# Attention and two feed-forward layers: k's parts, q's low part and a sum placed in other blocks, v's load behind k's moves, and one step of a weight's conversion a block sooner

## The chip, the cores and the metric

One Trainium2 chip, of which the program uses one core. The metric is the time of one launch in microseconds of device time, median of several runs. A core has TensorE (PE; its weight loads are PEld), VectorE (DVE), ScalarE (ACT), GpSimd (POOL) and SyncE (SP, which here only issues DMAs). Each works off its own list of instructions in order, and waits where an operand is not there yet.

## What is computed

Clustered attention over 2 x 8 heads of 768 positions and 64 dimensions: queries and keys get the nearest of 16 centroids, a query sees only the keys of its own centroid. Two feed-forward parts follow.

```python
mask = q_assign[:, :, :, None] == k_assign[:, :, None, :]
scores = np.where(mask, scale * np.matmul(q, k.transpose(0, 1, 3, 2)), -1000000000.0)
attn = softmax(scores)                      # exp(s - max) / (sum + 1e-9)
x = np.matmul(attn, v)                      # -> (1536, 512)
x = ((x @ w1) * (x @ w2)) @ w3 @ w_out
out = (sigmoid(x @ w_gate) * (x @ w_val)) @ w_out2
```

## The kernel before

Everything runs as float32 split in a high and a low part (`hi` and `lo`, in the engine's fast float32 format), so that a product takes two or three passes. The weights are loaded as raw words and rebuilt in several steps (`f64_steps`, "conversion"), each step on another engine.

The attention part is one loop over 48 blocks (L580 to L706). A block is 256 queries of one head; `i` counts blocks, six to a pair of heads, three a head. `pr` is the pair (0 to 7) and `at` the block in it (0 to 5). `nxt` is pair `pr + 1`, `later` is `pr + 2` (none from pr = 6 on). The order of all engines is the order of this code: the scheduler leaves it alone, so a call's place in the loop is its place in its engine's list.

In one turn PE computes the scores `s` of a later block (L339, twice), turns the exponentials of block i (`pt`, L372, three times) and multiplies block i - 1 with v (`av`, L413 with the high part `ph`, L414 with the low part `pl`, in three groups k2 = 0, 1, 2). DVE takes the maxima `nm` (L351) and most of the `pl` (L401). ACT takes the exponentials `e` (L362), the `ph` (L390) and copies `av` to `xa` (L422, `take_x`); all blocks share one `av`, so the next block's products wait for this copy. In blocks 0, 1, 2 and 4 ACT only copies `pt` to `pc` for k2 = 0 (L387) and POOL makes `ph` and `pl` from it (L54, L59).

Between these stand the steps that prepare the next pairs. They are bound to blocks by `if` lines:

- `load_qk(later)` at block 0; `raw` is q and k of a pair. `prep_split` (L185) makes four tiles of it: `hi0` (q, ACT, L192) at block 3, `lo0` (q, DVE, L194), `hi1` (k, ACT, L56) and `lo1` (k, POOL, L59) at block 4. Each has one buffer, which the pair before uses too.
- `prep_scatter` moves rows of them by DMA into the operands QH, KH, QX and KX: for the pair's first head at block 5 of `later`'s turn, for the second at block 1 of `nxt`'s turn, there behind `load_v(nxt)`.
- `join_x` (blocks 0 and 1) moves the halves of the last pair's result by DMA, `add_x` (POOL, L466, block 3) adds them, `spread` reads the sums' inverses `r` back by DMA, `norm_x` and `split_x` (POOL, block 5) finish x.
- The mask of the next pair: DVE turns the one-hot matrix (`ohT`, L282, end of block 2), and at block 3 eight small DMAs carry it into QH and KH (`prep_mask`). Behind them SP issues the two DMAs of `spread`.

The first-layer weights `w_0_0` and `w_0_1` are converted inside the attention part. `steps[1]` is that of `w_0_1`; its first step issues the load of `w_f` (L88), its second is a DVE operation on what was loaded (`w_a`, L100), then ACT, POOL and DVE again. `loads` (L656) and `CONVERT` (L572) say in which block (pr, at) a step is written: the load in (6, 4), the DVE step in (6, 5), the rest in pair 7.

Of the kernel before, what the change touches and what calls it, by code (L numbers as in the profile page):

```python
# [8 lines left out]
F32 = mybir.dt.float32  # L9
# [18 lines left out]
def tile_cluster_attention__then__moe__then__gated_moe(  # L28
# [22 lines left out]
    def split(x, hi, lo, hi_engine, lo_engine):  # L51

        if hi_engine is nc.gpsimd:
            nc.gpsimd.tensor_scalar(out=hi, in0=x, scalar1=1.0, scalar2=1.0, op0=ALU.mult, op1=ALU.mult)  # L54
        elif hi_engine is nc.scalar:
            nc.scalar.copy(hi, x)  # L56
        else:
            nc.vector.tensor_copy(hi, x)
        lo_engine.tensor_tensor(out=lo, in0=x, in1=hi, op=ALU.subtract)  # L59

    def move(dst, src):
        nc.sync.dma_start(dst.bitcast(F32), src.bitcast(F32))
# [109 lines left out]
    def load_v(pr, e=None):  # L172
        if e != 1:
            raw[pr, "v"] = core.tile([128, 2, KT, D], F32, tag="vraw", name=f"vraw{pr}", bufs=1)
        which = slice(0, 2) if e is None else slice(e, e + 1)
        nc.sync.dma_start(raw[pr, "v"][:, which], v[pr][:, which])
# [5 lines left out]

        return nc.vector if pr == 0 else nc.gpsimd

    def prep_split(pr):  # L185
        hl = []
        for w in range(2):
            t = raw[pr, w]
            hi = core.tile([128, S], F32R, tag="hi", name=f"hi{pr}_{w}", bufs=2)
            lo = core.tile([128, S], F32R, tag="lo", name=f"lo{pr}_{w}", bufs=2)  # L190
            if w == 0:
                nc.scalar.activation(hi, t, AF.Copy, scale=0.125)  # L192
                yield
                nc.vector.scalar_tensor_tensor(out=lo, in0=t, scalar=0.125, in1=hi.bitcast(F32), op0=ALU.mult, op1=ALU.subtract)  # L194
            else:
                split(t, hi, lo, nc.scalar, nc.vector if pr == 0 else nc.gpsimd)
            hl += [hi, lo]
        opnd[pr, "hl"] = hl

    def prep_split_1_hi(w):  # L200

# [22 lines left out]
    def prep_scatter_hi(pr, e):  # L224
        qh, ql, kh, kl = opnd[pr, "hl"]
        r = slice(64 * e, 64 * e + 64)
        QH, KH, QX, KX = operands(pr, e)
        move(QH[0:64], qh[r])
        move(KH[0:64], kh[r])
        move(QX[0:64], qh[r])  # L230
        move(KX[64:128], kh[r])

    def prep_scatter_lo(pr, e):
        qh, ql, kh, kl = opnd[pr, "hl"]
# [144 lines left out]
    def split_hi(i, k2):  # L379
        if (i, k2) not in pts:  # L380
            return
        pt = pts[i, k2]
        ph = core.tile([128, 2, 256], F32R, tag="ph", name=f"ph{i}_{k2}", bufs=4)
        pl = core.tile([128, 2, 256], F32R, tag="pl", name=f"pl{i}_{k2}", bufs=4)
        if by_pool(i, k2):
            pc = core.tile([128, 2, 256], F32, tag="pc", name=f"pc{i}", bufs=1)
            nc.scalar.copy(pc, pt)  # L387
            pts[i, k2] = pc
        else:
            nc.scalar.copy(ph, pt)  # L390
        phs[i, k2] = (ph, pl)
# [43 lines left out]
    def invert(pr):  # L435

        ss = acc_x[pr, "sum"]
        nc.vector.reciprocal(ss, ss)
# [133 lines left out]
    CONVERT = {}  # L572
    for n, slots in enumerate((
        ((0, 3), (0, 3), (0, 5), (1, 0), (1, 0), (1, 1)),
        ((6, 5), (7, 0), (7, 1), (7, 2), (7, 3), (7, 4)),
    )):
        for slot in slots:
            CONVERT.setdefault(slot, []).append(n)
    if True:
        for i in range(-2, NB + 2):  # L580
            pr, at = divmod(i, 6)
            nxt = pr + 1 if 0 <= i and pr + 1 < NPR else None
            later = nxt + 1 if nxt and nxt + 1 < NPR else None

            scores(2 * i + 3)
            if i == -1:
                warm(11, "warm3")
            split_hi(i - 1, 2)
            transposes(i, 0)
            if i == NB - 1:  # L590
                turn_sums(pr, ps_s.tile([128, 1024], F32, tag="s", name=f"rp{pr}")[:, 0:128])
            maxima(2 * i + 3)
            if i == 0:
                prep_code(0, 1)
                prep_onehot(0, 1)
                prep_turn(0, 1)
                prep_sims(1)
                prep_sum(1)
            if i == NB - 1:
                store_sums(pr)  # L600
            if later and at == 0 and pr:
                load_qk(later)
            if at == 0 and 0 < pr and i < NB:
                join_x(pr - 1, 0)
            if at == 1 and 0 < pr and i < NB:
                join_x(pr - 1, 1)
            if nxt and nxt > 1 and at == 1:
                load_v(nxt)
                prep_scatter_hi(nxt, 1)
                if nxt > 2:  # L610
                    prep_scatter_lo(nxt, 1)
            if nxt and at == 3:
                for e in range(2):
                    if nxt == e == 1:
                        prep_scatter(1, 1)
                    prep_mask(nxt, e)
                    if nxt == 2 and e == 0:
                        prep_scatter_lo(2, 1)
            split_lo(i - 1, 2)
            split_hi(i, 0)  # L620
            split_lo(i, 0)
            if i == 0:
                next(split_1_lo, None)
                prep_v(0, 1)
            if nxt and at == 1:
                prep_argmax(nxt)
            if nxt and at == 2:
                prep_onehot(nxt)
            if 0 < pr and i < NB and at == 5:
                norm_x(pr - 1)  # L630
                split_x(pr - 1)
            if nxt == 1 and at == 2:
                load_v(nxt)
            if 0 < pr and i < NB and at == 3:
                add_x(pr - 1)
                spread(pr - 1, "xb", 1)
            exponentials(2 * i + 3)
            if i == -1:
                next(split_1_lo)
                prep_argmax(0, 1)  # L640
                load_qk(2)
            if 0 <= i < NB and at == 4:
                guard_sums(pr)
            if later and at == 3:
                halves = prep_split(later)
                next(halves)
            if later and at == 4:
                for _ in halves:
                    pass
            weighted_v(i - 1, 0)  # L650
            weighted_v(i - 1, 1)
            if i == 1:
                prep_scatter(1, 0)
            if later and at == 5:
                prep_scatter(later, 0)
            loads = ((6, 4), (7, 1), (7, 3))  # L656
            if (pr, at) in loads:
                convert(1 + loads.index((pr, at)))

            similar = later if at == 5 else None  # L660
            if similar:
                prep_sims(similar)
            scores(2 * i + 4)
            turning = 0 <= i < NB - 1 and at == 5
            if turning:
                turn_sums(pr, sps[2 * i + 4][:, S : S + 128])
            if nxt and at == 1:
                prep_code(nxt)
            if 0 < pr < NPR and at == 0:
                prep_v(pr, 1)  # L670
            if nxt and at == 3:
                prep_v(nxt, 0)
            transposes(i, 1)
            split_hi(i, 1)
            weighted_v(i - 1, 2)
            transposes(i, 2)
            if i == NB:
                convert(2)
            take_x(i - 1)
            if i == NB:  # L680
                convert(3)
            if i == 0:
                prep_mask(0, 1)
            if similar:
                prep_sum(similar)
            maxima(2 * i + 4)
            if turning:
                store_sums(pr)
            if nxt == 1 and at == 2:
                prep_turn(nxt)  # L690
            if i == NB - 2:
                invert(pr)
            for n in CONVERT.get((pr, at), ()):
                convert(n)
            split_lo(i, 1)
            if nxt and nxt > 1 and at == 2:
                prep_turn(nxt)
            exponentials(2 * i + 4)
            if 0 <= i < NB - 2 and at == 4:
                invert(pr)  # L700
            if i == NB - 2:
                end_move(0)
            if i == NB:
                end_move(1, FIRST)
                spread(END, "raw", 4)
                end_add(0)  # L706
        end_move(1, LAST)
        end_add(1, FIRST)
        end_norm(FIRST)
        end_split(FIRST)  # L710
        end_add(1, LAST)
        end_norm(LAST)
        end_split(LAST)
# [551 lines left out]
```

## Time and profile before

| | before |
|---|---|
| median of 3 runs | 750.98 us (750.78 to 752.79) |
| profiled execution, its own time | 749.76 us |
| its span | 747.8 us |
| PE busy | 740.3 us, 99% of the span |
| DVE, ACT, POOL busy | 575.0, 473.1, 414.8 us (77%, 63%, 55%) |
| chain that ended last | PE 89%, DMA, ACT and DVE 2% each |

The attention part fills the first 228 us, the rest is matrix products without a break. A matmul's record is longer than the time that it takes from its neighbours: matmuls of 256 columns are recorded as 0.28 us and start 0.12 us apart. So a busy PE can hide a wait of up to 0.16 us, and waits are read from the distance of starts. In a timeline the columns are start (us), length (us), engine, line, operation, out<-in with shapes, count; behind it in brackets the idle time ahead of it and what ended it.

### The profile page before, as it was taken

How to read it: one execution, taken by the hardware profiler on the slowest of the kernel's cores; microseconds unless marked ns; L12 is line 12 of the kernel's file. 1: busy time of each engine (PE TensorE's matmuls, PEld its weight loads, DVE VectorE, ACT ScalarE, POOL GpSimd, SP SyncE). 2: the span in 40 equal slices, each digit the busy share in tenths (PEclk: the TensorE clock that was granted, in tenths of full speed). 3: DMA queues.
4: the chain of work that ended last, by engine and by line, in shares of the span. 5: the costliest groups of instructions: out<-in, count | busy, mean ns of one | idle time of the engine just before them, and what ended most of it. 6: DMA issues, size and time to landing. Idle time of an engine off the chain costs nothing.

```text
span 747.8 us, 12291 instructions
## 1 busy us (share of the span) xinstructions
PE 740.3 (99%) x4270; PEld 670.4 (90%) x4270; DVE 575.0 (77%) x893; ACT 473.1 (63%) x994; POOL 414.8 (55%) x420
## 2 busy tenths in 40 slices
PE   8999999999999999999999999999999999999998
PEld 7888998998998888888889999999999999999996
DVE  7999999999987677676743486685686968869675
ACT  8988989888894555645522356777656564565630
POOL 4777878878682755424321037775647555475510
PEclk9999999999999999999999999999999999999999
DMA  6777686676432434433420000221303113030004
GB/s 197 179 192 173 181 208 165 172 183 168 111 110 89 153 129 140 142 113 118 150 99 1 1 29 28 86 85 57 114 2 115 53 57 114 29 113 29 30 0 169
DMA packets 29054, 80.10 MB, mean 107 GB/s; under 512 B 5056, under 2 KB 6656, under 8 KB 28992
## 3 DMA queue, kind: packets, MB, share of 16 engines
q1 hardware_dynamic: 28992, 79.32, 35.8%
q8 instruction: 34, 0.56, 0.3%
q14 instruction: 28, 0.23, 0.1%
HBM read 52.46 MB, written 3.19 MB: 74 GB/s over the span
## 4 chain that ended last, share of the span: by engine, by line
PE 89%; DMA 2%; ACT 2%; DVE 2%; POOL 1%; issue 1%; SPq 1%; POOLq 0%; DVEq 0%; ACTq 0%
PE p L67 13%; PE p L66 13%; PE p L65 13%; PE s L339 6%; PE pt L372 6%; PE p_a L66 4%; PE p_a L67 4%; PE p_a L65 4%; PE av L413 3%; PE av L414 3%; PE p_b L65 2%; PE p_b L66 2%; PE p_b L67 2%; PE w34p L67 2%; PE w34p L66 2%; PE w34p L65 2%
## 5 line engine op out<-in xcount | busy, mean ns | idle before, releaser
L362 ACT ACTIVATE e<-s,nm 128x768 f32<-128x768 f32 x96 | 88.3, 920 | 13.0 <-DVE nm L351 12.6
L351 DVE TENSOR_REDUCE nm<-s 128x1 f32<-128x768 f32 x96 | 90.5, 944 | 6.7 <-PE s L339 6.2
L372 PE MATMUL pt<-ident,e 128*128 128x128 f32 x576 | 86.0, 272 | 0.2 <-DVE sm L255 0.2
L413 PE MATMUL av<-ph,vx 128*128 128x256 f32 x288 | 81.2, 308 | 0.6 <-POOL pl L59 0.2
L401 DVE TENSOR_TENSOR pl<-pt,ph 128x512 fp32r<-128x512 f32 x113 | 75.8, 683 | 5.6 <-ACT ph L390 4.4
L67 PE MATMUL p<-x,w 128*128 128x512 f32 (+1 forms) x208 | 80.1, 385 | 0.0
L66 PE MATMUL p<-x,w 128*128 128x512 f32 (+1 forms) x208 | 80.1, 385 | 0.0
L65 PE MATMUL p<-x,w 128*128 128x512 f32 (+1 forms) x208 | 80.0, 385 | 0.0
L414 PE MATMUL av<-pl,vx 128*128 128x256 f32 x288 | 74.7, 288 | 0.7 <-DVE pl L401 0.5
L116 POOL TENSOR_TENSOR w_a<-w_f 128x512 uint32<-128x512 uint32 x30 | 32.1, 1070 | 76.2 <-DVE w_f L115 38.0
L390 ACT CAST ph<-pt 128x512 fp32r<-128x512 f32 x113 | 64.6, 590 | 13.4 <-PE pt L372 13.0
L372 PEld LDWEIGHTS pt<-ident,e 128*128 128x128 f32 x576 | 67.7, 141 | 4.5 <-DVE sm L255 0.5
L1144 DVE TENSOR_TENSOR acc<-p,acc 128x512 f32<-128x512 f32 x59 | 40.5, 687 | 29.3 <-PE p L67 29.2
L960 POOL TENSOR_TENSOR wgv_a<-wgv_f 128x512 uint32<-128x512 uint32 x24 | 25.3, 1053 | 66.7 <-DVE wgv_f L959 38.4
L1038 ACT COPY s<-p_a 128x384 f32<-128x384 f32 x72 | 34.4, 478 | 43.2 <-PE p_a L67 42.8
L67 PE MATMUL p<-wo,u 128*128 128x512 f32 (+1 forms) x146 | 57.3, 393 | 0.0
L414 PEld LDWEIGHTS av<-pl,vx 128*128 128x128 f32 x288 | 54.5, 189 | 3.0 <-DVE pl L401 2.2
L66 PE MATMUL p<-wo,u 128*128 128x512 f32 (+1 forms) x146 | 57.1, 391 | 0.0
L413 PEld LDWEIGHTS av<-ph,vx 128*128 128x128 f32 x288 | 54.4, 189 | 2.7 <-POOL pl L59 1.3
L65 PE MATMUL p<-wo,u 128*128 128x512 f32 (+1 forms) x146 | 56.3, 386 | 0.0
L339 PE MATMUL s<-KH,QH 80*128 80x512 f32 x192 | 54.5, 366 | 1.3 <-ACT e L362 0.8
L339 PE MATMUL s<-KX,QX 128*128 128x512 f32 x192 | 49.6, 340 | 0.0
(254 smaller groups left out, 2220.9 us busy)
## 6 DMA issues: line engine op xcount, KB each, us to landing
wgv_f<-in_w_gv_dram SPq DMA_DIRECT2D x24, 512.0 KB, 3.2
wo_f<-in_w_out_dram SPq DMA_DIRECT2D x20, 512.0 KB, 3.1
w_f<-in_w_dram SPq DMA_DIRECT2D x16, 512.0 KB, 3.3
w_f<-in_w3T_dram SPq DMA_DIRECT2D x16, 512.0 KB, 3.2
raw<-in_qkT_dram SPq DMA_DIRECT2D x16, 384.0 KB, 4.7
r<-r_dram SPq DMA_DIRECT2D x16, 192.0 KB, 4.1
xb<-xa SPq DMA_DIRECT2D x15, 192.0 KB, 3.3
out_dram<-acc SPq DMA_DIRECT2D x11, 256.0 KB, 2.0
```

The costliest lines, as they stand in the source:

```text
L65: nc.tensor.matmul(ps, whi, xhi, start=start, stop=False, skip_group_check=more)
L66: nc.tensor.matmul(ps, whi, xlo, start=False, stop=False, skip_group_check=more)
L67: nc.tensor.matmul(ps, wlo, xhi, start=False, stop=stop, skip_group_check=more)
L339: nc.tensor.matmul(sp[:, c], products[n][0], products[n][1][:, c], start=n == 0, stop=n == 1)
L351: nc.vector.tensor_reduce(out=nms[j], in_=sps[j][:, 0:S], axis=AX.X, op=ALU.max, negate=True)
L362: nc.scalar.activation(et, sps.pop(j)[:, 0:S], AF.Exp, bias=nms.pop(j), accum_out=acc_x[pr, "sum"][:, at : at + 1])
L372: nc.tensor.transpose(pt[:, kk, 128 * t : 128 * t + 128], exps[2 * i + t][:, k0 : k0 + 128], ident)
L390: nc.scalar.copy(ph, pt)
L401: nc.vector.tensor_tensor(out=pl, in0=src, in1=ph, op=ALU.subtract)
L413: nc.tensor.matmul(avs[i], w, ph[:, kk, :], start=kt == 0, stop=False)
L414: nc.tensor.matmul(avs[i], w, pl[:, kk, :], start=False, stop=kt == KT - 1)
L1144: nc.vector.tensor_tensor(out=acc[:, t, :], in0=bk, in1=acc[:, t, :], op=ALU.add)
```

## The change

Five things are done, all inside the attention loop.

1. `prep_split` is cut into single steps. From later = 3 on (pr = 1 to 5) k's high part `hi1` (ACT) goes from block 4 to the end of block 2, and q's low part `lo0` (DVE) from the middle of block 4 to its end. From pr = 2 on k's low part `lo1` (POOL) goes from block 4 to block 3.
2. `add_x` (POOL) goes from block 3 to block 2, ahead of that block's `ph` and `pl`, for pr = 2 to 5.
3. In the scatter of pairs 2 and up, k's two high moves go ahead of q's.
4. v's load goes behind k's two moves.
5. In `loads` the load of `w_0_1` is written in (6, 3), and in `CONVERT` its DVE step in (6, 4).

```diff
-    def prep_split(pr):
...
+    def split_tiles(pr):
+        opnd[pr, "hl"] = [core.tile([128, S], F32R, tag=tag, name=f"{tag}{pr}_{w}", bufs=2) for w in range(2) for tag in ("hi", "lo")]
+
+    def split_hi_q(pr):
+        nc.scalar.activation(opnd[pr, "hl"][0], raw[pr, 0], AF.Copy, scale=0.125)
+
+    def split_lo_q(pr):
+        scaled_lo(opnd[pr, "hl"][1], raw[pr, 0], opnd[pr, "hl"][0])
+
+    def split_hi_k(pr):
+        nc.scalar.copy(opnd[pr, "hl"][2], raw[pr, 1])
+
+    def split_lo_k(pr):
+        nc.gpsimd.tensor_tensor(out=opnd[pr, "hl"][3], in0=raw[pr, 1], in1=opnd[pr, "hl"][2], op=ALU.subtract)
...
-        move(QH[0:64], qh[r])
-        move(KH[0:64], kh[r])
-        move(QX[0:64], qh[r])
-        move(KX[64:128], kh[r])
+        parts = [(QH[0:64], qh), (KH[0:64], kh), (QX[0:64], qh), (KX[64:128], kh)]
+        if pr > 1:
+            parts = parts[1::2] + parts[0::2]
+        for n, (to, part) in enumerate(parts):
+            if n == 2 and pr > 1 and e == 1:
+                load_v(pr)
+            move(to, part[r])
...
-        ((6, 5), (7, 0), (7, 1), (7, 2), (7, 3), (7, 4)),
+        ((6, 4), (7, 0), (7, 1), (7, 2), (7, 3), (7, 4)),
...
             if nxt and nxt > 1 and at == 1:
-                load_v(nxt)
                 prep_scatter_hi(nxt, 1)
...
             split_hi(i, 0)
+            if 0 < pr and i < NB and at == (2 if later and pr > 1 else 3):
+                add_x(pr - 1)
             split_lo(i, 0)
...
-                add_x(pr - 1)
                 spread(pr - 1, "xb", 1)
...
-                halves = prep_split(later)
-                next(halves)
+                if not pr:
+                    split_tiles(later)
+                split_hi_q(later)
             if later and at == 4:
-                for _ in halves:
-                    pass
+                if not pr:
+                    split_lo_q(later)
+                    split_hi_k(later)
+                if pr < 2:
+                    split_lo_k(later)
...
-            loads = ((6, 4), (7, 1), (7, 3))
+            loads = ((6, 3), (7, 1), (7, 3))
...
+            if later and at == 3 and pr > 1:
+                split_lo_k(later)
...
             take_x(i - 1)
+            if later and at == 2 and pr:
+                split_tiles(later)
+                split_hi_k(later)
...
+            if later and at == 4 and pr:
+                split_lo_q(later)
```

DVE's list in pair 6, blocks 4 and 5, before. Here `nm_3294` is the second maximum of block 4's turn, `pl_1_3281` and `pl_2_3307` the low parts of block 4, `rt` stands at the end of block 5.

```order
L351 TENSOR_REDUCE nm_3294<-s_3270 128x1
L401 TENSOR_TENSOR pl_1_3281<-pt_1_3275,ph_1_3280 128x512
L438 RECIPROCAL ss_2865<-ss_2865 128x12
L351 TENSOR_REDUCE nm_3314<-s_3301 128x1
L401 TENSOR_TENSOR pl_2_3307<-pt_2_3287,ph_2_3306 128x512
L401 TENSOR_TENSOR pl_0_3318<-pt_0_3309,ph_0_3317 128x512
L351 TENSOR_REDUCE nm_3358<-s_3334 128x1
L453 COPY rt_3360<-s_3334 12x128
L100 TENSOR_SCALAR w_0_1_a<-w_0_1_f_3267 128x512
L401 TENSOR_TENSOR pl_1_3346<-pt_1_3340,ph_1_3345 128x512
```

And now:

```order
L354 TENSOR_REDUCE nm_3294<-s_3270 128x1
L100 TENSOR_SCALAR w_0_1_a<-w_0_1_f_3203 128x512
L404 TENSOR_TENSOR pl_1_3281<-pt_1_3275,ph_1_3280 128x512
L441 RECIPROCAL ss_2864<-ss_2864 128x12
L354 TENSOR_REDUCE nm_3315<-s_3302 128x1
L404 TENSOR_TENSOR pl_2_3308<-pt_2_3287,ph_2_3307 128x512
L404 TENSOR_TENSOR pl_0_3319<-pt_0_3310,ph_0_3318 128x512
L354 TENSOR_REDUCE nm_3359<-s_3335 128x1
L456 COPY rt_3361<-s_3335 12x128
L404 TENSOR_TENSOR pl_1_3347<-pt_1_3341,ph_1_3346 128x512
```

The step on `w_0_1` has moved ahead of seven instructions, the first of which makes the low part of block 4's second group.

SP's list at the same place, now: the last two mask moves of block 3, the two reads of `r`, the load, and the store of block 5.

```order
L62 DMA QH_1_3033<-ohT_None 16x384
L62 DMA KH_1_3034<-ohT_None 16x384
L464 DMA r_3190<-r_dram 64x768 x2
L88 DMA w_0_1_f_3203<-in_w_dram 128x1024
L457 DMA r_dram<-rt_3361 12x128
```

The list of before has the same DMAs in the same order here; the load's place among them has not moved.

POOL's list in pair 3, blocks 1 to 4, before (`sm` is the end of block 1, the first `ph` and `pl` are block 2's, `vx` splits v, the second `ph` and `pl` are block 4's):

```order
L271 TENSOR_TENSOR sm_1618<-sm_1618,dec 128x384
L54 TENSOR_SCALAR ph_0_1792<-pc_1794 128x512
L59 TENSOR_TENSOR pl_0_1793<-pc_1794,ph_0_1792 128x512
L301 TENSOR_SCALAR ohT_None<-ohT_None 64x384
L466 TENSOR_TENSOR xa_0_1328<-xa_0_1328,xb_1647 128x768
L54 TENSOR_SCALAR vx_0_1892<-vraw_1714 128x6x64
L59 TENSOR_TENSOR vx_0_1892<-vraw_1714,vx_0_1892 128x6x64
L54 TENSOR_SCALAR ph_0_1934<-pc_1936 128x512
L59 TENSOR_TENSOR pl_0_1935<-pc_1936,ph_0_1934 128x512
L59 TENSOR_TENSOR lo_1_1945<-raw_1_1645,hi_1_1944 128x768
```

And now:

```order
L274 TENSOR_TENSOR sm_1618<-sm_1618,dec 128x384
L469 TENSOR_TENSOR xa_0_1328<-xa_0_1328,xb_1647 128x768
L54 TENSOR_SCALAR ph_0_1792<-pc_1794 128x512
L59 TENSOR_TENSOR pl_0_1793<-pc_1794,ph_0_1792 128x512
L304 TENSOR_SCALAR ohT_None<-ohT_None 64x384
L54 TENSOR_SCALAR vx_0_1895<-vraw_1720 128x6x64
L59 TENSOR_TENSOR vx_0_1895<-vraw_1720,vx_0_1895 128x6x64
L198 TENSOR_TENSOR lo_1_1838<-raw_1_1645,hi_1_1837 128x768
L54 TENSOR_SCALAR ph_0_1938<-pc_1940 128x512
L59 TENSOR_TENSOR pl_0_1939<-pc_1940,ph_0_1938 128x512
```

`xa` stands ahead of block 2's `ph` instead of behind it, and `lo_1` ahead of block 4's `ph`.

## Rows read from the trace of the kernel before

**Rows 1.** Windows: busy us (count) of each engine, granted clock, DMA.

```profile
100.00:150.00 50.00, 49.84 (x382) 45.79 (x381) 47.42 (x68) 43.90 (x97) 40.21 (x36) 1.00 0.69 178
```

**Rows 2.** Timeline, SP, pair 6, from the first mask move to the load.

```profile
191.62 0.55 SPq L62 DMA_DIRECT2D QH<-ohT_None  x1
196.71 2.04 SPq L461 DMA_DIRECT2D r<-r_dram  x2
198.79 0.58 SPq L88 DMA_DIRECT2D w_f<-in_w_dram  x1
```

**Rows 3.** The chain that ended last, same stretch: start, us, what.

```profile
198.79 3.93 DMA w_f<-in_w_dram
```

**Rows 4.** Timeline, DVE, pair 6.

```profile
191.03 0.57 DVE L282 STREAM_TRANSPOSE ohT_None<-oh 128x384 f32<-128x384 f32 x1
196.98 0.96 DVE L351 TENSOR_REDUCE nm<-s 128x1 f32<-128x768 f32 x1 [0.26 <-PE s L339]
202.75 1.23 DVE L100 TENSOR_SCALAR w_a<-w_f 128x512 uint32<-128x512 uint32 x1 [0.37 <-DMA w_f<-in_w_dram]
```

**Rows 5.** Timeline, PE, pair 6, blocks 5 and 0.

```profile
199.75 0.28 PE L413 MATMUL av<-ph,vx 128*128 128x256 f32 x1
199.87 0.28 PE L414 MATMUL av<-pl,vx 128*128 128x256 f32 x1
204.00 0.28 PE L413 MATMUL av<-ph,vx 128*128 128x256 f32 x1
204.63 0.39 PE L414 MATMUL av<-pl,vx 128*128 128x256 f32 x1 [0.36 <-DVE pl L401]
```

**Rows 6.** Timeline, POOL, pair 6.

```profile
201.85 1.84 POOL L470 TENSOR_TENSOR xa<-xa,r 128x768 f32<-128x768 f32 x1 [3.29 <-DMA r<-r_dram]
```

**Rows 7.** Instructions of L100: duration ns min/median/max, first and last start.

```profile
L100 DVE TENSOR_SCALAR w_a<-w_f x2: 405/819/1233, 33.3 to 202.7; 128x512 uint32<-128x512 uint32 x2
```

**Rows 8.** DMAs issued by L88.

```profile
DMA to landing us min/median/max: 3.2/3.3/5.2
```

**Rows 9.** Timeline, ACT, pair 3, end of block 2 and of block 4.

```profile
110.65 0.90 ACT L362 ACTIVATE e<-s,nm 128x768 f32<-128x768 f32 x1 [0.55 <-DVE nm L351]
117.96 0.84 ACT L56 CAST hi<-raw 128x768 fp32r<-128x768 f32 x1
119.18 0.38 ACT L422 COPY xa<-av 128x256 f32<-128x256 f32 x1
```

**Rows 10.** Timeline, PE, pair 3, blocks 3 and 5.

```profile
110.98 0.34 PE L414 MATMUL av<-pl,vx 128*128 128x256 f32 x1
118.95 0.60 PE L372 MATMUL pt<-ident,e 128*128 128x128 f32 x4
119.70 0.35 PE L413 MATMUL av<-ph,vx 128*128 128x256 f32 x1 [0.15 <-ACT xa L422]
```

**Rows 11.** Timeline, POOL, pair 3.

```profile
103.91 1.27 POOL L59 TENSOR_TENSOR pl<-pc,ph 128x512 fp32r<-128x512 f32 x1
108.55 0.62 POOL L54 TENSOR_SCALAR ph<-pc 128x512 fp32r<-128x512 f32 x1 [1.85 <-PE s L339]
109.25 1.64 POOL L59 TENSOR_TENSOR pl<-pc,ph 128x512 fp32r<-128x512 f32 x1
112.44 1.86 POOL L466 TENSOR_TENSOR xa<-xa,xb 128x768 f32<-128x768 f32 x1
```

**Rows 12.** Timeline, SP, and DMA issues by line (KB each, us to landing).

```profile
104.48 0.46 SPq L62 DMA_DIRECT2D xa<-xa  x1
...
xb<-xa SPq DMA_DIRECT2D x15, 192.0 KB, 3.3
```

**Rows 13.** Timeline, PE, first stretch, and a window at the end.

```profile
1.51 3.46 PE L137 MATMUL warm<-ident 128*128 128x128 f32 x15 [1.51 <-POOL ident masks.py:199]
6.51 3.27 PE L137 MATMUL warm<-ident 128*128 128x128 f32 x28
...
744.60:747.80 3.20, 0.03 (x1) 0.00 (x0) 0.42 (x1) 0.00 (x0) 0.00 (x0) 1.00 0.47 164
```

More of the change, by code (lines that the diff above doesn't have):

```diff
@@ L183, in lead @@
         return nc.vector if pr == 0 else nc.gpsimd
-    def prep_split(pr):
[L186 to L198, printed above, removed]
+    def split_tiles(pr):
[8 more added lines that the diff above has]
+        nc.gpsimd.tensor_tensor(out=opnd[pr, "hl"][3], in0=raw[pr, 1], in1=opnd[pr, "hl"][2], op=ALU.subtract)
     def prep_split_1_hi(w):
```

## The prediction

> **What bounds the kernel now.** I read the windows first, then the timelines of PE and of whoever releases it, then the chain of waits. In the attention part PE is busy 49.84 of 50 us, with DVE at 47.4, ACT at 43.9 and POOL at 40.2 [rows 1]. So PE sets the pace there, and DVE has some 5% in hand: what holds DVE for long reaches PE. Since a busy PE can hide a wait, I read its waits from starts. Products of one group start 0.12 us apart (199.75, 199.87); at 204.00 the next one starts only at 204.63, held for 0.51 us by a low part from DVE [rows 5]. That low part stood behind the DVE step on `w_0_1`, which started at 202.75, the moment its load had landed, and took 1.23 us [rows 4]. The chain of waits runs through that load [rows 3]. In pair 3 PE lost time in the same way to ACT: its transposes from 118.95 end at 119.55, the products behind them start at 119.70, since the copy of `av` that they need ended at 119.56; 0.15 us are listed, and as much as 0.16 more can be hidden (0.28 us recorded for a start every 0.12), so 0.3 us [rows 5, 9, 10]. Waits of this kind are all that can be won, well under 1 us a pair.
>
> **The change: the step on the weight.** Written two lines earlier, the load is not issued earlier. SP's list is the same there: eight mask moves, two reads of `r`, then the load. The moves start when DVE has turned the one-hot matrix (191.03 plus 0.57, first move at 191.62), the reads follow at 196.71, the load at 198.79 [rows 2, 4], and it lands 3.93 us later, at 202.72 [rows 3]. It waited for nothing but its place, so (6, 3) or (6, 4) is the same to it.
>
> The DVE step is what moves. It now stands right behind the second maximum of block 4, which runs from 196.98 to 197.94 [rows 4]. There DVE must wait until 202.72: 4.8 us. Queued behind it are the low part of block 4's second group, the reciprocal, a maximum, two low parts, another maximum and the copy `rt`. PE needs the first of these at 199.87 [rows 5]. When does it get it? Landing 202.72, the step 1.23 us from 202.75, which gives 203.98; the step can run in 0.41 us [rows 7], but POOL's `norm_x` runs from 201.85 to 203.69 as before [rows 6], since the reads of `r` have not moved, so I keep 1.23. In the trace of before the same low part behind the same step released PE at 204.63 [rows 5]. The arithmetic is the same now, for the group that PE wants at 199.87: a loss of 204.63 - 199.87 = 4.76 us.
>
> What comes back: the 0.51 us of today's wait, because the step no longer stands in block 5. Is something else late next? Before, DVE did all that now stands behind the step between 197.94 and 202.38 (the step's start less its 0.37 us of idle time), 4.44 us with its own waits in it [rows 4]. From 203.98 on that ends by 208.42, and block 5's low part 0.65 us later (203.98 to 204.63), at 209.07 at the latest. PE wants it when it has done 204.00 + 0.12 - 199.87 = 4.25 us of its own work from 204.63 on, at 208.88 [rows 5]. So at most 0.2 us more, and none if DVE's waits in the 4.44 fall away; I take none. Term: **+4.25 us** (4.76 - 0.51). Ends: the two reads took 2.04 us to issue where two moves take 1.27 (eight from 191.62 to 196.71), and the fastest load of this line landed after 3.2 us, which together would bring the landing 1.5 us forward (0.8 and 0.7): +2.7. The slowest took 5.2 us [rows 2, 8]: +5.5.
>
> On POOL's share in that 1.23 us: the row shows the step ending 0.29 us after `norm_x` did, and 0.41 us when alone [rows 4, 6, 7]. The Trainium skill (SBUF — State Buffer, "SBUF: two separate sides") says that VectorE and GpSimd share one pair of ports as an exclusive lock, held for a whole instruction, against VectorE operations with two SBUF inputs or in a two-port mode. The trace agrees; without that rule the term would be 3.4.
>
> **The change: the five steps of the pairs.** *k's high part* (ACT, 0.84 us) leaves block 4, where ACT runs without a break and its copy at 119.18 comes late, for the end of block 2, where ACT has 0.55 us idle before 110.65 [rows 9]. That idle time covers most of it; up to 0.3 us is carried through block 3. If the two moves that read the tile's last contents had not landed it would hold ACT; they now go right behind the move at 104.48, ahead of v's load, so an estimate is 3.3 us, as for their sister move, behind issues 0.6 and 1.2 us after it: 109.0 for the later one, before ACT is free at 110.1 [rows 9, 12]. This is worth between 0 and the 0.3 us of pair 3 in each of five pairs; I take 0.2, nearer to the row, so **-1.0 us**.
>
> *q's low part* (DVE) stays in its block and has the same work ahead of it by its new place; two maxima and low parts come sooner, the next maximum not later. I put it at nothing; in pair 1, where POOL's `lo1` stays in block 4, the two can meet, at most one POOL operation of 1.86 us [rows 11], of which DVE's slack takes most; this goes into the range.
>
> *`add_x`* on POOL, 1.86 us [rows 11], now runs ahead of block 2's `ph` and `pl`. POOL was idle there for 1.85 us before 108.55, so from 106.70. But `add_x` needs the move issued at 104.48 [rows 12]. If it has landed by 106.70, `ph` starts at 108.56 as before, a loss of 0. If it takes 3.3 us, like its sister move, `add_x` ends at 109.64 and `pl` 1.09 us later than its 110.89; some 0.37 of that comes back, since the 1.64 us of that `pl` were 1.27 alone [rows 11]. PE takes it at 110.98 with no slack [rows 10]: a loss of up to 0.75 us. Four pairs, each between 0 and 0.75; I take the middle, 0.35, so **+1.4 us**.
>
> *`lo1`* in block 3 takes the room that `add_x` leaves, and *the order of the moves* changes no amount of data: v's load lands later by two moves of 0.6 us issue, and POOL's `prep_v` comes behind `ph` and `pl` of block 2. Both at nothing.
>
> The sum: +4.25 - 1.0 + 1.4 = +4.65 us. Against the profiled execution (749.76, span 747.8) that is 754.4; carried to the median of the runs, 750.98, it is **755.6 us**. Behind the attention part everything is a list of products without a break, which shifts as a whole.
>
> **The rivals.** *The clock falls in the new wait.* PE would stand still from about 200.0 to 204.6. The first 15 transposes of the program take 3.46 us, later 28 take 3.27 [rows 13]: half the pace, the two levels 1.2 and 2.4 GHz, after PE had done nothing. Against it: the last window has a granted clock of 1.00 through 3.2 us with next to no matmul [rows 13]. No row shows 4.6 us. If it fell and came back after as long a stretch as at the start, 3.4 us at half pace cost 1.7, less the little that DVE is late anyway: 1.5, so 757.1. The Trainium skill (TensorE: Matmul & The Clock Gate, "HAM oscillation — how this bites in real kernels") says that waits which leave TensorE idle bring its clock down and that the work behind them starts slow.
>
> *POOL becomes the bound in blocks 2 and 3.* `add_x` at its worst in four pairs (3.0 for 1.4) and no gain on ACT: 755.6 + 1.6 + 1.0 = 758.2. For it speaks that PE takes POOL's `pl` without slack at 110.98; against it that POOL had 1.85 us idle there.
>
> *Not slower: the wait is hidden.* PE wants the low part at 199.87. Less 0.41 for the step and 0.65 for the low part, a landing up to 198.8 would cost nothing; that is the point from which it decides. Then today's 0.51 us goes and the pairs count -1.0 to +1.4: 750.98 - 0.51 + 0.4 = 750.9, and 749.5 with the gain alone. It needs SP to reach the load 3.9 us sooner, that is, six of the eight mask moves gone from ahead of it, and the order shows all eight. That the load does what its name says, and comes sooner, is this same rival.
>
> **How the numbers follow.** Forecast 755.6: 0.55. Clock falls, 757.1: 0.20. POOL bound, 758.2: 0.08. A short wait, with the reads and the load at their fastest and the pairs winning, 750.98 + 2.7 - 1.0 = 752.7: 0.10. Hidden, 749.5 to 750.9: 0.07. The range leaves out the hidden wait and the ends of the others: 752.7 to 758.2. A measurement of this kernel can tell some 0.3%, 2.25 us, from no change. Slower than 753.2: the first three cases and a third of the fourth, 0.86. Faster than 748.7: the outermost part of the last, 0.02. Within: 0.12.
>
> **What would show it.** In the new profile the waits should list PE behind DVE's low part with one wait of 4 to 5 us near 200, and DVE's step behind the load with an idle time of 4 to 5 us, where it had 0.37; the load's issue some 7 us behind the one-hot transpose, as now. PE's products at block 5 of pairs 1 to 5 should follow their transposes after 0.35 us; those of block 3 in pairs 2 to 5 should show a wait for POOL's `pl`. A load that issues well before the reads of `r`, or a DVE idle time under 1 us there, would make the prediction wrong; transposes 0.21 us apart behind the wait would show the clock.

## The result, and the profile after

| | before | after |
|---|---|---|
| median of 6 runs | 750.99 us (749.76 to 752.79) | 758.49 us (757.98 to 760.07) |
| profiled execution, its own time | 749.76 us | 760.07 us |
| its span | 747.8 us | 758.3 us |
| mean granted TensorE clock there | 1.000 | 0.995 |

The changed kernel is slower: the ratio is 1.010, with a 95% interval of 1.0085 to 1.0114, that is, +7.5 us. The forecast was 755.6 us, the upper end of its range 758.2. The direction was right; the time lies 0.3 us above the range, and 2.9 us above the forecast. The profiled execution is the longest of the six.

The page of the changed kernel; the digits of PEclk are the granted clock in 40 slices of the span, in tenths:

```profile
PE 743.7 (98%) x4270; PEld 673.0 (89%) x4270; DVE 574.7 (76%) x893; ACT 474.4 (63%) x994; POOL 411.7 (54%) x420
...
PEclk9999999999989999999999999999999999999999
```

One slice, the twelfth (208.5 to 227.5 us), shows an 8. Before, all forty show a 9. PE is recorded as busy 3.4 us longer than before (740.3) with the same work: part of its work ran at half pace.

The waits of the changed kernel, by engine, line and what was waited for (total us, times, longest us). The first two lines are of the whole program, the others of 40 to 200 us, pairs 1 to 6:

```profile
DVE w_a L100 <- DMA w_f<-in_w_dram: 4.8, 1, 4.8
...
PE av L417 <- DVE pl L404: 4.7, 2, 4.6
```

```profile
PE av L416 <- ACT xa L425: 1.4, 2, 0.8
PE pt L375 <- DVE pl L404: 1.0, 1, 1.0
PE av L417 <- POOL pl L59: 0.5, 2, 0.4
```

The first fence is the weight step, as forecast. The second is the pairs: of its three lines the forecast expected only the one with POOL's `pl`.

SP in pair 6 (answers to [rows 2]):

```profile
195.26 0.55 SPq L62 DMA_DIRECT2D QH<-ohT_None  x1
...
200.35 1.97 SPq L464 DMA_DIRECT2D r<-r_dram  x2
202.37 0.58 SPq L88 DMA_DIRECT2D w_f<-in_w_dram  x1
```

DVE there (answers to [rows 4]):

```profile
200.99 0.96 DVE L354 TENSOR_REDUCE nm<-s 128x1 f32<-128x768 f32 x1 [0.53 <-PE s L342]
206.75 1.18 DVE L100 TENSOR_SCALAR w_a<-w_f 128x512 uint32<-128x512 uint32 x1 [4.81 <-DMA w_f<-in_w_dram]
```

PE there (answers to [rows 5]):

```profile
203.75 0.28 PE L416 MATMUL av<-ph,vx 128*128 128x256 f32 x1
208.59 0.58 PE L417 MATMUL av<-pl,vx 128*128 128x256 f32 x1 [4.55 <-DVE pl L404]
208.97 0.41 PE L416 MATMUL av<-ph,vx 128*128 128x256 f32 x1
209.18 0.41 PE L417 MATMUL av<-pl,vx 128*128 128x256 f32 x1
```

The load has kept its place, 7.11 us behind the first mask move (7.17 before). DVE stands 4.81 us, PE's next product starts 4.84 us after the one before it instead of 0.12: 4.72 us lost. And what the forecast's main case did not have: behind the wait products start 0.21 us apart (208.97, 209.18). The windows of the same stretch (us, then busy us and count of PE, PEld, DVE, ACT, POOL, then the granted clock, DMA share, GB/s):

```profile
206.00:208.00 2.00, 0.00 (x0) 0.00 (x0) 1.25 (x2) 0.00 (x0) 1.91 (x2) 0.88 0.01 4
...
212.00:214.00 2.00, 2.00 (x10) 1.90 (x10) 0.96 (x3) 1.75 (x5) 0.00 (x0) 0.50 0.05 12
214.00:216.00 2.00, 2.00 (x17) 1.96 (x16) 1.24 (x2) 1.38 (x5) 0.13 (x1) 0.92 0.40 89
```

0.12, 0.08 and three windows at 0.50 make 2 x (0.12 + 0.08 + 1.50) = 3.4 us of lost clock, so 6.8 us at 1.2 GHz, from 207.5 to 214.3. PE worked through 5.7 us of it, which cost 2.85 us. So in this execution: 4.72 - 0.51 for the wait, 2.85 for the clock, and 3.64 us by which the first mask move of pair 6 is late (195.26 against 191.62), which is the pairs' share: 10.7 us, where the own times differ by 10.3.

### The profile page after: what moved, and what is told of

It is laid out like the page before. It is cut to its first block, busy times and chain, and to the rows that moved or that the text cites. A ratio compares the mean times of both kernels' runs of the same rounds, so it can differ in the third digit from the quotient of the medians.

```text
span 758.3 us, 12277 instructions
## 1 busy us (share of the span) xinstructions
PE 743.7 (98%) x4270; PEld 673.0 (89%) x4270; DVE 574.7 (76%) x893; ACT 474.4 (63%) x994; POOL 411.7 (54%) x420
## 4 chain that ended last, share of the span: by engine, by line
PE 86%; DVE 4%; ACT 3%; issue 2%; DMA 2%; POOL 1%; SPq 0%; DVEq 0%; POOLq 0%; ACTq 0%
PE p L67 13%; PE p L66 13%; PE p L65 13%; PE s L342 6%; PE pt L375 5%; PE p_a L66 4%; PE p_a L67 4%; PE p_a L65 4%; PE av L417 3%; PE av L416 3%; PE p_b L65 2%; PE p_b L66 2%; PE p_b L67 2%; PE w34p L67 2%; PE w34p L66 2%
```

## The experiments

Each kernel was timed beside the kernel before, whose median was 750.3 to 750.7 us there; not all of them ran on the same chip. The gains and losses below are therefore the ratio, times 751, and differences between two experiments are differences of ratios.

### The weight step alone

```diff
-        ((6, 5), (7, 0), (7, 1), (7, 2), (7, 3), (7, 4)),
+        ((6, 4), (7, 0), (7, 1), (7, 2), (7, 3), (7, 4)),
...
-            loads = ((6, 4), (7, 1), (7, 3))
+            loads = ((6, 3), (7, 1), (7, 3))
```

> The kernel before with part 5 alone (load of w_0_1 written in (6, 3), DVE's step in (6, 4)). Theory 1, wait and clock: PE stands some 4.5 to 4.8 us ahead of the low part near 200 us, less the 0.51 us of before (+4.25), and its transposes behind the wait start 0.21 us apart for about 6 us, which costs 1 to 3 us more: 756.3 to 758.2 us, mean granted clock below 1.000. Theory 2, wait alone, as the forecast had it: 755.2 us and a clock of 1.000. Theory 3, the pairs' steps carry the loss: under 753.5 us.

756.18 us, ratio 1.0076 (1.0058 to 1.0094): +5.7 us, short of the 756.3 by 0.1 us and with the falling clock of theory 1. Three executions have a mean granted clock of 0.998 (754.34 to 756.17 us), three of 0.995 (756.19 to 758.27); none has the 0.999 or 1.000 of the kernel before. PE in the profiled one, which is of the first kind:

```profile
199.51 0.28 PE L413 MATMUL av<-ph,vx 128*128 128x256 f32 x1
203.59 0.39 PE L414 MATMUL av<-pl,vx 128*128 128x256 f32 x1 [3.80 <-DVE pl L401]
203.81 0.28 PE L413 MATMUL av<-ph,vx 128*128 128x256 f32 x1
203.93 0.28 PE L414 MATMUL av<-pl,vx 128*128 128x256 f32 x1
...
206.41 0.41 PE L413 MATMUL av<-ph,vx 128*128 128x256 f32 x1
206.62 0.41 PE L414 MATMUL av<-pl,vx 128*128 128x256 f32 x1
```

Its windows:

```profile
204.00:206.00 2.00, 2.00 (x12) 1.76 (x11) 2.00 (x4) 0.99 (x2) 1.54 (x1) 0.63 0.00 0
206.00:208.00 2.00, 2.00 (x10) 2.00 (x10) 1.42 (x3) 1.51 (x3) 0.00 (x0) 0.52 0.01 3
```

The wait is over at 203.59, the first products behind it are 0.12 us apart, and then the clock falls all the same: 2 x (0.37 + 0.48) = 1.7 us of lost clock, that is, 3.4 us at half pace, from about 204.5 to 207.9. That it comes with the wait is to be seen here; that it comes from PE's idleness is for the next two.

### PE kept at work during the wait

The first try put 36 transposes into unused columns of a score tile:

```diff
+            if (pr, at) == (6, 5):
+                for _ in range(36):
+                    nc.tensor.transpose(idle_room, ident, ident)
             weighted_v(i - 1, 1)
```

> weight_only with 36 transposes of the identity added in pair 6, block 5, ahead of the products that wait for DVE's low part; their result lands in unused columns of a score tile and nobody reads it. At 0.117 us each (28 in 3.27 us) they take 4.2 us, which fits in the wait of 4.7. Theory 1 (the clock falls because PE stands idle): the same wait of DVE for the load, but the granted clock stays at 1.000 and the time is that of weight_only less 1 to 3 us, 755.2 us. Theory 2 (the clock has no part in it): the time of weight_only within 0.5 us, or longer if the transposes get in the way.

761.82 us (1.0163; 1.0143 to 1.0182), which does not decide between the theories, since PE stood idle in this kernel too:

```profile
205.17 6.36 PE L655 MATMUL s<-ident 128*128 128x128 f32 x36 [5.93 <-ACT e L362]
```

The transposes themselves had to wait for the exponentials that read the same tile, so PE stood 5.93 us ahead of them, and then they took 6.36 us, 0.18 us each, since the clock had fallen (0.50 from 204 to 208 us, 0.57 from 208 to 210). The second try puts 30 of them into the unused half of the tile of `av`, ahead of block 4's products:

```diff
+            if (pr, at) == (6, 5):
+                for _ in range(30):
+                    nc.tensor.transpose(words["room"][:, 0:128], ident, ident)
             weighted_v(i - 1, 0)
```

> weight_only with 30 transposes of the identity ahead of block 4's products in pair 6, block 5; their result lands in the unused half of the tile that holds av, where nothing waits for them and nobody reads them. At 0.117 us each they take 3.5 us of the 3.96 us that PE lost to the wait in weight_only. DVE's wait for the load is as in weight_only in both theories. Theory 1 (the clock falls because PE stands idle): the granted clock stays at 1.00 behind the wait, products start 0.12 us apart there, and the time is about 1.7 us below that of weight_only (half pace through some 3.4 us there), 754.5 us. Theory 2 (idleness has no part in it): the same low clock, the time within 0.5 us of weight_only.

754.46 us, ratio 1.0052 (1.0036 to 1.0068), 1.7 us below weight_only. DVE and PE:

```profile
204.29 0.47 DVE L100 TENSOR_SCALAR w_a<-w_f 128x512 uint32<-128x512 uint32 x1 [5.82 <-DMA w_f<-in_w_dram]
```

```profile
199.81 3.44 PE L652 MATMUL av<-ident 128*128 128x128 f32 x30
...
205.42 0.38 PE L414 MATMUL av<-pl,vx 128*128 128x256 f32 x1 [1.58 <-DVE pl L401]
205.64 0.28 PE L413 MATMUL av<-ph,vx 128*128 128x256 f32 x1
205.76 0.28 PE L414 MATMUL av<-pl,vx 128*128 128x256 f32 x1
```

Its window behind that:

```profile
206.00:208.00 2.00, 2.00 (x19) 1.88 (x17) 2.00 (x4) 1.60 (x4) 1.39 (x1) 1.00 0.00 0
```

DVE's wait is there and even longer, PE stands still for 1.58 us, but the clock stays at 1.00 and products start 0.12 us apart; none of the twelve executions has a mean clock under 0.999. So the low clock came from PE's standing still. One thing is not shut out: weight_only ran on another chip, and nothing without the transposes and with as long a wait of PE was run on this one. (The half pace of the program's first transposes, 15 in 3.46 us, is in both traces.) By the medians the clock costs about 1.8 us of the 5.7 (1.0076 against 1.0052) and the wait itself 3.9, where the forecast's term was 4.25. Both sizes are rough. The two intervals overlap, and in the profiled executions PE lost 4.9 us to the transposes and the rest of the wait here, against 4.0 to the wait in weight_only, so the clock may have cost up to 1 us more.

### The load really sooner

```diff
+            if (pr, at) == (6, 3):
+                convert(1)
             if nxt and at == 3:
                 for e in range(2):
...
-        ((6, 5), (7, 0), (7, 1), (7, 2), (7, 3), (7, 4)),
+        ((6, 4), (7, 0), (7, 1), (7, 2), (7, 3), (7, 4)),
```

> The kernel before with the load of w_0_1 issued in (6, 3) ahead of the eight mask moves, and DVE's step in (6, 4) as in the changed kernel. Theory 1 (what counts is the place in SP's list): the load issues about 7 us sooner and lands by 196, ahead of the step; no wait of DVE, the 0.51 us of before are gone, 0 to -0.5 us: 750.2 us where before has 750.7. Theory 2 (the step's new place in DVE's list is wrong by itself): a wait of PE for DVE's low part near 200 remains, 751.5 us or more. Rival: the mask, now behind a load of 512 KB, comes too late for pair 7's scores, which would show as a wait of PE for KH or QH near 216 us.

750.32 us, ratio 0.9996 (0.9979 to 1.0013): no difference that can be told. SP and DVE:

```profile
189.93 0.66 SPq L88 DMA_DIRECT2D w_f<-in_w_dram  x1
191.92 0.55 SPq L62 DMA_DIRECT2D QH<-ohT_None  x1
```

```profile
198.61 0.53 DVE L100 TENSOR_SCALAR w_a<-w_f 128x512 uint32<-128x512 uint32 x1
```

The same DVE step in the same place waits for nothing once the load stands ahead of the mask moves, and PE waits for nothing from 180 to 220 us. So it was the load's place in SP's list, and nothing about the step's own place, that cost the 5.7 us. What the forecast called the hidden wait is this kernel, not the one under study.

### The pairs' steps without the weight step

> The changed kernel without part 5 (load and DVE step of w_0_1 back in (6, 4) and (6, 5)). Theory A, from the trace of the changed kernel: the steps of pairs 1 to 5 cost PE about 3.6 us up to pair 6 in that execution, in pair 1 and pair 4 above all: 752.5 to 754.6 us. Theory B, the forecast's sum of -1.0 and +1.4: 751.4 us. Rival: they win, 750 us, and the whole loss was the weight's.

752.57 us, ratio 1.0029 (1.0016 to 1.0043): +2.2 us, theory A at its lower end, with a clock of 1.00. With the 5.7 of weight_only this makes 7.9, against 7.5 for both: the two halves of the change add up, within what the intervals can tell. PE's waits from 40 to 200 us:

```profile
PE av L417 <- POOL pl L59: 1.3, 3, 0.6
PE pt L375 <- DVE pl L404: 0.9, 1, 0.9
PE av L416 <- ACT xa L425: 0.7, 1, 0.7
```

Three causes, one run or two for each.

**`add_x`.** Part 2 alone:

> The kernel before with part 2 alone: add_x in block 2, ahead of that block's ph and pl, for pairs 2 to 5. Theory (add_x has to wait for the move of xa, and pushes POOL's low part past the moment at which PE wants it): waits of PE for POOL's pl in pairs 3 to 5, 0.4 to 0.8 us each, about 2.0 us in all, the forecast's term having been 1.4 of 0 to 3.0: 752.1 to 752.7 us. Rival (these waits show only beside the other steps): 750.5 us and no such wait.

751.68 us, ratio 1.0017 (1.0000 to 1.0034): +1.3 us, under the 2.0 expected, with an interval that reaches down to no loss at all, and in pairs 2 and 3 rather than 3 to 5. POOL, and PE's waits from 40 to 200 us:

```profile
81.86 1.84 POOL L466 TENSOR_TENSOR xa<-xa,xb 128x768 f32<-128x768 f32 x1 [0.80 <-DMA xa<-xa]
...
109.79 1.85 POOL L466 TENSOR_TENSOR xa<-xa,xb 128x768 f32<-128x768 f32 x1 [1.64 <-DMA xa<-xa]
```

```profile
PE av L414 <- POOL pl L59: 1.5, 2, 1.0
```

Where the move of `xa` lands late, `add_x` holds POOL's `pl` and PE with it; in pairs 4 and 5 it landed in time here.

**q's low part beside `lo1`.** In pair 1 `lo1` has stayed in block 4. DVE and POOL of the changed kernel there, and PE behind them:

```profile
67.25 2.31 DVE L218 SCALAR_TENSOR_TENSOR lo<-raw,hi 128x768 fp32r<-128x768 f32 x1
```

```profile
66.90 1.84 POOL L198 TENSOR_TENSOR lo<-raw,hi 128x768 fp32r<-128x768 f32 x1
```

```profile
69.93 0.27 PE L450 MATMUL s<-ident,ss 128*12 128x128 f32 x1
71.17 0.63 PE L375 MATMUL pt<-ident,e 128*128 128x128 f32 x4 [0.97 <-DVE pl L404]
```

Putting q's low part of pair 1 back (`if pr < 2: split_lo_q(later)` in its old place):

> pairs_only with q's low part of pair 1 alone at its old place in block 4. Theory (in pair 1 it meets POOL's lo1, which has stayed in block 4): the step takes 1.36 us again instead of 2.3, PE's 1.09 us at the transposes of block 5 are gone and block 5's old wait of 0.4 us for xa is not back: 751.6 us. Rival (pair 1's loss comes from k's high part): the 1.09 us remain in another place, 752.6 us.

751.98 us (1.0019; 1.0002 to 1.0036). The step takes 1.35 us and the wait at the transposes is gone; of its 1.1 us some 0.7 show between the ratios, but the intervals overlap, so the times alone don't show it. The sharper test lets the two meet in every pair, by giving POOL its old list and leaving q's low part in its new place:

```diff
-            if 0 < pr and i < NB and at == (2 if later and pr > 1 else 3):
+            if 0 < pr and i < NB and at == 3:
                 add_x(pr - 1)
...
-                if pr < 2:
-                    split_lo_k(later)
+                split_lo_k(later)
...
-            if later and at == 3 and pr > 1:
-                split_lo_k(later)
```

> pairs_only with POOL's list as in the kernel before: add_x in block 3 and k's low part lo1 in block 4 of every pair; q's low part stays at the end of block 4. Theory (add_x costs PE 2.0 us at POOL's low parts of pairs 3 to 5; q's low part and lo1 slow each other wherever both stand in block 4): the waits for POOL's pl are gone, -2.0, but the 1.09 us of pair 1 appear in pairs 2 to 5 too, up to +4.4: 755.0 us where pairs_only has 752.6, and L218 takes about 2.3 us in five pairs instead of one. Rival (what pair 1 shows is peculiar to it): 750.6 us.

757.15 us (1.0087; 1.0068 to 1.0106), 4.4 us above pairs_only. DVE's step by line (count, busy us and mean ns of one), and PE's wait:

```profile
L218 DVE SCALAR_TENSOR_TENSOR lo<-raw,hi 128x768 fp32r<-128x768 f32 x5 | 11.2, 2240 | 0.0
```

```profile
PE pt L375 <- DVE pl L404: 3.4, 5, 1.0
```

2.24 us in all five pairs, and PE waits in all five; the time is 2 us more than expected, for which the listed waits do not account in full. So the pair matters: the new place of q's low part does no harm only because `lo1` has left block 4, and in pair 1 it has not. In pairs 2 to 5 of the changed kernel the step meets nothing of POOL's and takes 0.90 us, as here in pair 3, where POOL is idle from 121.54 to 124.50:

```profile
121.85 0.90 DVE L218 SCALAR_TENSOR_TENSOR lo<-raw,hi 128x768 fp32r<-128x768 f32 x1
```

So the 1.35 us of the kernel before, and of pairs_lo_back, are not the step alone: it ran beside POOL's `ph` and `pl` there, and that `pl` took 1.86 us instead of 1.28. The Trainium skill (SBUF — State Buffer, "SBUF: two separate sides") has the two engines exclude each other for a whole instruction, where VectorE has two inputs in SBUF and GpSimd reads SBUF. The trace agrees: DVE ends 0.82 us behind POOL in pair 1 (69.56 and 68.74 above), about the 0.90 that the step takes alone.

**The order of the moves.** Undoing parts 3 and 4 within pairs_only:

> pairs_only with parts 3 and 4 undone: q's moves and k's in the old order, v's load ahead of them. Theory A1, q's high part on ACT waits in pairs 1 and 4 until the last move that reads its tile has landed, since that move now stands behind k's moves and v's load: without these parts ACT's idle time ahead of q's high part (0.58 us in pair 1, 1.46 us in pair 4) is gone and the time is 1.5 to 2 us below pairs_only. Theory A2, k's high part at the end of block 2 delays ACT by itself: the time of pairs_only within 0.5 us, and k's high part, whose tile is now read later, waits instead.

758.67 us (1.0117; 1.0097 to 1.0137), against theory A1. ACT, and PE's waits:

```profile
59.41 0.83 ACT L195 CAST hi<-raw 128x768 fp32r<-128x768 f32 x1 [2.60 <-DMA KX<-hi]
```

```profile
PE s L338 <- ACT e L361: 6.7, 5, 2.4
```

k's high part in its new place overwrites the tile that the move to KX still reads, so it waits up to 2.6 us when that move goes last. Parts 3 and 4 are needed for part 1. (The time also holds a fall of the clock, of which the last section tells: the five executions have mean clocks of 0.995 to 0.998.) The price for them shows when they stand alone in the kernel before:

> The kernel before with parts 3 and 4 alone (k's two moves first, then v's load, then q's two). Theory A (q's moves behind v's load land late, and ACT's q high part has to wait for them): ACT waits ahead of L192's high part in pair 4, perhaps in pair 1, by 0.5 to 1.5 us, and the time is 0.5 to 1.9 us above before, 751.2 to 752.6 us. Rival (the order is free as long as k's high part stays in block 4): 750.7 us and no such wait.

752.11 us (1.0019; 1.0006 to 1.0033): +1.4 us. But not by theory A: ACT has no wait ahead of q's high part. PE waits for the mask instead:

```profile
PE s L342 <- DMA KH<-ohT_None: 1.0, 2, 0.5
```

In the changed kernel there is a wait of the other form: in pair 4 ACT's q high part waits for a DMA, and PE for ACT's copy. The DMA that the profile names is a move of the mask, which neither reads nor writes the tile of q, so which one it was isn't shown.

```profile
143.70 0.85 ACT L189 ACTIVATE hi<-raw 128x768 fp32r<-128x768 f32 x1 [1.46 <-DMA QH<-ohT_None]
```

```profile
145.34 0.39 PE L416 MATMUL av<-ph,vx 128*128 128x256 f32 x1 [0.80 <-ACT xa L425]
```

With v's load behind all four moves:

> pairs_only with v's load behind all four moves of the operands instead of behind k's two. Theory A1 (q's moves land late because v's load is ahead of them): ACT's wait ahead of q's high part in pair 4 (1.42 us) is gone, and PE's 0.94 us there; POOL's split of v may wait instead: 751.6 us where pairs_only has 752.6. Theory A2 (it is the second place behind k's moves): the wait remains, within 0.3 us of pairs_only.

752.34 us (1.0020; 1.0001 to 1.0038): ACT's wait is gone, and a wait of PE for the mask of 0.5 us is there in its place, so the time is that of pairs_only within the intervals. That v's load caused ACT's wait is not shown by this: in pair 4 of pairs_lo_back and pairs_pool_back, which have the order of pairs_only, the wait is missing too. Why one of these DMAs lands late and not another, and why not in every profile, stays open; what is shown is that reordering them is not free.

### What shows a gain, put together

> What the profiles show to win, put together: the kernel before with k's high part at the end of block 2, the new order of moves that it needs, and the load of w_0_1 ahead of the mask moves with DVE's step in (6, 4); POOL's list and q's low part as before. Theory: the waits for xa in block 5 (0.4 us in three of the pairs) and the 0.5 us of pair 6 are gone, the wait of q's high part in pair 4 stays: 750.7 - 1.2 - 0.4 + 0.9 = 750.0 us. Rival (k's high part at the end of block 2 costs more than it brings): 751 us or more.

751.57 us (1.0009; 0.9994 to 1.0025). The waits for `xa` in block 5 are gone, but PE waits 1.0 us for the mask:

```profile
PE s L342 <- DMA KH<-ohT_None: 1.0, 1, 1.0
```

> k_high_load_first with v's load behind all four moves. Theory: ACT's waits ahead of the high parts are gone too, 749.1 us, under 750.0. Rival: v's load, now last, makes POOL's split of v or the mask moves behind it late, and the gain is lost: 750 us or more.

751.53 us (1.0012; 0.9998 to 1.0025), the rival's case. Neither beats the kernel before. No wait for POOL's `pl` from 40 to 200 us is left in k_high_load_first, which fits with `add_x` having caused those of pairs_only.

## Why the prediction was right and wrong, point by point

- **The load's place in SP's list**: right. Load 7.11 us behind the first mask move, DVE 4.81 us behind it in waiting where 4.8 was forecast, the step at 1.18 us beside `norm_x` where 1.23 was kept. The term was 4.25 us; in the trace of the changed kernel it measured 4.72 - 0.51 = 4.21, and by the medians with PE kept at work, roughly, 3.9.
- **The clock: the step that failed.** The fall was a rival at 0.20, it came in every execution of weight_only and of the changed kernel. What misled was the last row of [rows 13], 3.2 us with next to no matmul at 1.00. That row ends with the program: it can't show a fall that follows later. In weight_only the fall came 0.9 us after PE was at work again. And a granted clock of 1.00 alone is no proof of full pace: the window from 2 to 4 us of the same trace reads 1.00 too, while the transposes of [rows 13] take 0.23 us each there, twice their later time. Its price, 1.5 us, was nearly right for the short kind (1.7), and too small for the changed kernel's 2.85. The Trainium skill's rule (TensorE: Matmul & The Clock Gate, "HAM oscillation — how this bites in real kernels"), cited there beside the rival, agrees in direction, and weight_pe_kept_busy shows it from the other side. By it the work behind the wait starts slow: so it was in the changed kernel (208.97, 209.18), not in weight_only (203.81, 203.93).
- **`add_x`**: +1.4 forecast, +1.3 measured (the interval runs from 0 to 2.6), by the mechanism named (the move of `xa`), though not in all four pairs. The forecast's own terms give 1.09 - 0.37 = 0.72 us for the worst pair, where it has 0.75; this changes nothing.
- **k's high part**: -1.0 forecast. No run holds it alone, since it needs the moves. The waits for `xa` in block 5 are gone as forecast. The other terms as measured are +1.3, +1.4 and +0.7, the whole is +2.2, which leaves -1.2, an estimate of mine from these four. The other way round it is less: k_high_load_first (+0.7) less moves_only (+1.4) and load_first (-0.3) leaves -0.4. Each of these numbers is uncertain by 1 us or more, so that this term is a gain at all is not shown.
- **q's low part: a term of the wrong size.** The meeting with `lo1` in pair 1 was named, and left to the range, with DVE's slack to take most of it. PE lost 1.1 us where the step had grown by 0.95: DVE had no slack there at all. Some 0.7 us of it show between the ratios, not clear of the intervals. That the step would shrink to 0.90 us in the other pairs was not foreseen, and no gain from it shows.
- **The order of the moves: the other step that failed.** "Both at nothing" was argued from the amount of data. What counts is when each lands: +1.4 us alone (the interval runs from 0.5 to 2.5), with PE waiting for the mask.
- **The sum.** The forecast had +4.25 and +0.4, in all +4.65. Measured: +3.9 for the wait, +1.8 for the clock, +2.2 for the pairs, 7.9, against 7.5 for the changed kernel. The clock (1.8) and the pairs' moves and low part (1.4 and 0.7) are what the forecast had as a rival or at nothing; the other terms take some 0.7 us off, and that the parts don't add up quite takes 0.4 more, which leaves the miss of 2.9. Both happened at once, which no case of the forecast held: its case with the clock alone, 757.1 us, lies inside the range.

## What to carry to other kernels

A load is sooner when it issues sooner: read its place in the list of the engine that issues it, and move it there, before the step that needs it is moved. A wait that stops TensorE can cost more than its length, since work behind it can run at half pace: here it did in every execution of weight_only and of the changed kernel (waits of 3.80 and 4.55 us in their profiles). Count such a fall into the forecast, not among its rivals. And a DMA moved to the front moves others to the back: name for each of them who overwrites or reads what it carries.

## What was not expected of the hardware

The clock can fall after the wait is over: in weight_only PE was at work again from 203.59, and products were at full pace till past 203.93. The low stretch came in two sizes: weight_only has mean clocks of 0.998 and 0.995 on one chip, and in the two profiles, weight_only's at 0.998 and the changed kernel's at 0.995, it lasted 3.4 and 6.8 us. It followed a shorter wait too: in pairs_old_moves PE's wait of 2.4 us, ended at 61.18 us, was followed by

```profile
62.00:64.00 2.00, 2.00 (x15) 2.00 (x14) 1.79 (x3) 2.00 (x5) 0.52 (x1) 0.67 0.89 199
64.00:66.00 2.00, 2.00 (x10) 1.80 (x9) 1.27 (x2) 1.83 (x5) 0.00 (x0) 0.50 0.17 47
```

while a wait of 1.58 us in weight_pe_kept_busy was not followed by a low clock, nor was any wait of pairs_pool_back, the longest of which was 1.0 us.
